# Another order of the seven products, and of their three banks, in the first half of a feed-forward block

## The chip, the cores and the metric

The kernel runs on one core of one Trainium2 chip. A core has five engines with a queue of instructions each: PE (TensorE, matrix products), DVE (VectorE), ACT (ScalarE), POOL (GpSimd) and SP (which here only issues transfers). A product's result goes to PSUM, a small memory of eight banks that PE writes and that ACT and DVE read[...]. The metric is the time of one execution on the device in microseconds (us); lower is better.

## The reference

Thresholded attention (8 sequences, 8 heads, 576 tokens, 64 numbers a head), then a feed-forward block with an ELU between its two products. All data are 32-bit floats.

```python
scores = scale * np.matmul(q, k.transpose(0, 1, 3, 2))
thresh = np.max(scores, axis=-1, keepdims=True) - tau
scores = np.where(scores >= thresh, scores, -1000000000.0)
attn = np.exp(scores - np.max(scores, axis=-1, keepdims=True))
attn = attn / (np.sum(attn, axis=-1, keepdims=True) + 1e-09)
x = (attn @ v)          # then (B,H,S,D) -> (B*S, H*D) = 4608 x 512

h = x @ w_in            # 512 x 2048
g = np.where(h > 0.0, h, alpha * (np.exp(np.minimum(h, 0.0)) - 1.0))
out = g @ w_out         # 2048 x 512
```

## The kernel before, in words

Attention comes in 32 pairs of heads, each in five steps of up to 128 query rows. A step's scores go to PSUM (line 238); DVE takes the row maximum (line 1070); POOL makes the threshold from it (1074); ACT the exponential's bias and the exponential (1078 and 1080); DVE masks and sums (1089) and takes the reciprocal (1095, 1096); POOL normalizes (274). DVE and transfers turn the weights round (348, 361), and PE multiplies them with the values (384, 388).

The feed-forward block is computed in groups of 512 tokens. From the second group on, both its products use a scheme with seven half-size products in place of eight. One group takes eight units of the first product (the function `first_product(g, u)`), with a second round (`second_round`) after each four. A unit multiplies two blocks of 128 hidden columns with 2 x 256 tokens: seven short products, each of two matrix multiplications that appear as four records of 128x256 on PE (line 847). They go to three banks, called place 0, 1 and 2 in the code: `three` takes the next three banks from the list `ends`, and `ends.extend(...)` says in which order the next unit gets them. Until the attention ends there are three such banks for all units (`ends` holds just these); in the tail after it there are six.

In the order before, with k the number of the product (its slot) in the unit:

- k = 0, 1, 2 start places 0, 1 and 2. After each of them ACT copies the bank out (line 861: w, u, s), and POOL adds the copies up (line 866).
- k = 3 adds to place 0, and ACT copies the result out (line 906); k = 4 adds to place 1, and ACT copies it out (line 907). POOL makes t from that copy (line 866, t<-g,u).
- k = 5 adds a21 times x6 to place 0. DVE adds the bank to s and has one quarter of the hidden values (line 869, g<-f,s: the s-add).
- k = 6 adds a12 times x7 to place 2. DVE adds it to t and has the last quarter (line 869, g<-f,t: the t-add).

Adding to a bank doesn't clear it: a place goes on with the sum that it holds, and the copy in between reads what it holds so far. So a product that adds to a place must wait until the copy out of this place is done. The quarters are joined in pairs, halves c = 0 and c = 1. `exp(1)` takes the exponential of half 1 (line 875), and POOL subtracts one (line 889); `exp(0)` takes it of half 0 (line 875), and ACT subtracts one (line 880). Then DVE makes the ELU (line 895) and POOL sums of blocks (line 932), which the second round reads. The t-add completes half 0, the s-add half 1.

What sets the order of all this: the engines' queues are filled in the order in which the program text calls them. An agenda orders it: `on_pe` puts work on PE and advances a clock by a planned cost (0.87 us for a product), and `at(t, f)` puts a follow-up into the agenda at a planned time. The list `after_` holds for each product its follow-ups with their lags behind the product's end. These times only decide the order in each queue; on the chip an instruction starts when its engine is free and what it waits for is done. The attention steps put their work into the same agenda, so a changed lag can move an instruction past the softmax of a step.

In the second round the third product of a part reuses the bank of the first, which ACT copies out before (line 996).

Of the kernel before, what the change touches and what calls it, by code (L numbers as in the profile page):

```python
# [19 lines left out]
def kernel(  # L20
# [436 lines left out]
    def bank():  # L457
        return psum["f"].tile([P, 512], FP32, name="f", tag="f")
# [219 lines left out]
    def blocks_in(u):  # L678
        f0, f1 = (slice(f * P, (f + 1) * P) for f in (u, NU + u))
        return w_in_sb[:, :2, f0], w_in_sb[:, 2:, f0], w_in_sb[:, :2, f1], w_in_sb[:, 2:, f1]  # L680
# [65 lines left out]
    with tc.manual_schedule():  # L746
# [51 lines left out]
        def at(t, f):  # L798
            serial[0] += 1
            heapq.heappush(agenda, (t, serial[0], f))  # L800
# [15 lines left out]
        ends = [bank() for _ in range(3)]  # L816
# [3 lines left out]
        def kept(name):  # L820
            return epool.tile([P, HM], FP32, name=name)
# [4 lines left out]
        def first_product(g, u):  # L826
            r, v = divmod(u, RU)
            (b11, b12), (b21, b22) = ([xts[g][:, k : k + 2, t : t + CT] for t in (0, CT)] for k in (0, 2))
            a11, a12, a21, a22 = blocks_in(u)
            x1, x6, x7 = in_sums["x", g]  # L830
            loc = {}

            def product(k):
                if k == 0:
                    three = [ends.pop(0) for _ in range(3)]
                    ends.extend((three[1], three[0], three[2]))
                    loc["banks"] = [x[:, :CT] for x in three]
                    loc["s"] = in_sums.pop(u)
                    if v == 0:
                        for c in range(2):  # L840
                            gs[g, r, c] = more[r, c] if (r, c) in more else gpool.tile([P, RU, 2, 2, P], FP32, name="g", bufs=2)
                s = loc["s"]
                left, right, place, begins = ((s[:, 1], b22, 0, True), (s[:, 2], b11, 1, True), (s[:, 0], x1, 2, True),
                                              (a11, b12, 0, False), (a22, b21, 1, False), (a21, x6, 0, False),
                                              (a12, x7, 2, False))[k]
                for j in range(2):
                    nc.tensor.matmul(loc["banks"][place], left[:, j], right[:, j], start=(begins and j == 0), stop=(j == 1),  # L847
                                     skip_group_check=True)

            def h(j, c):  # L850
                return gs[g, r, c][:, v, j].rearrange("p i t -> p (i t)")

            def both(c):
                return gs[g, r, c][:, v].rearrange("p j i t -> p (j i t)")

            def place(x):
                return loc["banks"][x]

            def copy(name, x):
                loc[name] = kept(name)  # L860
                nc.scalar.copy(loc[name], place(x))  # L861

            def pool(name, x, other, op):
                if name not in loc:
                    loc[name] = kept(name)
                nc.gpsimd.tensor_tensor(loc[name], x(), loc[other], op)  # L866

            def add(o, x, name):
                nc.vector.tensor_tensor(o, place(x), loc[name], ALU.add)  # L869

            def exp(c):
                while len(late_elus) > 1:
                    late_elus.pop(0)[1]()
                e = loc["e", c] = late["x"].tile([P, 2 * CT], FP32, name="ge", bufs=2)
                nc.scalar.activation(e, both(c), AF.Exp)  # L875
                if c:
                    loc["e1"] = e
                    at(now[0] + 0.75, minus)
                else:
                    nc.scalar.activation(e, e, AF.Copy, bias=-1.0)  # L880
                if attending[0] and (v < RU - 1 or c):
                    late_elus.append((now[0] + 0.7 * c, lambda: elu(c)))
                else:
                    at(now[0] + 1.4, lambda: elu(c))

            def minus():
                e = loc.pop("e1", None)
                if e is not None:
                    nc.gpsimd.tensor_scalar(e, e, 1.0, -1.0, ALU.mult, ALU.add)

            def elu(c):
                if c:
                    minus()

                nc.vector.scalar_tensor_tensor(both(c), loc["e", c], 0.0, both(c), ALU.min, ALU.max)  # L895
                ready.add((g, r, c, v))
                if v % 2:
                    sums(g, r, c, v - 1)

            nm = lambda x: lambda: loc[x]  # L900
            after_ = (
                [(0.1, lambda: copy("w1", 0))],
                [(0.1, lambda: copy("u2", 1)), (0.55, lambda: pool("u2", nm("u2"), "w1", ALU.add))],
                [(0.1, lambda: copy("s1", 2)), (0.6, lambda: pool("s1", nm("s1"), "u2", ALU.subtract)),
                 (0.15, lambda: next_in(g, u))],
                [(0.1, lambda: nc.scalar.copy(h(0, 1), place(0)))],  # L906
                [(0.1, lambda: nc.scalar.copy(h(1, 0), place(1))),
                 (0.55, lambda: pool("t5", lambda: h(1, 0), "u2", ALU.subtract))],
                [(0.1, lambda: add(h(1, 1), 0, "s1")), (1.4 if attending[0] else 0.7, lambda: exp(1))],
                [(0.1, lambda: add(h(0, 0), 2, "t5")), (0.7, lambda: exp(0))],  # L910
            )
            return [(lambda k=k: product(k), after_[k]) for k in range(7)]

        def next_in(g, u):
            x = first_order.index((g, u)) + 2
            if x < len(first_order):
                load_in(first_order[x][1])

        def sums(g, r, c, v):
            def one(k):  # L920
                gt = gs[g, r, c][:, v : v + 2]
                (a11, a21), (a12, a22) = ([gt[:, :, j, i] for i in range(2)] for j in range(2))
                if (r, c, k) in more:
                    cur[g, r, c, k] = more[r, c, k]
                if (g, r, c, k) not in cur:
                    cur[g, r, c, k] = late["x"].tile([P, RU, P], FP32, name=f"s{k}", bufs=1 if k else 2)
                s1, s2, s3, s4 = (cur.get((g, r, c, x)) for x in range(4))
                s1, s2, s3, s4 = (x if x is None else x[:, v : v + 2] for x in (s1, s2, s3, s4))
                o, x, y, op = ((s1, a21, a22, ALU.add), (s2, s1, a11, ALU.subtract),
                               (s3, a11, a21, ALU.subtract), (s4, a12, s2, ALU.subtract))[k]  # L930
                engine = nc.gpsimd if attending[0] or k == 2 else nc.vector
                engine.tensor_tensor(o, x, y, op)  # L932

            for k in range(4):
                job = (0.8, (g, r, c, k), lambda k=k: one(k))

                if c and k and (r, c, k) not in more and (g, r, k) not in ready:
                    waiting.setdefault((g, r, k), []).append(job)
                else:
                    extra.append(job)  # L940
# [108 lines left out]
        def group(g):  # L1049
            for r in range(2):  # L1050
                for u in range(RU * r, RU * r + RU):
                    queue.append((first_product, (g, u)))
                queue.append((second_round, (g, r)))
# [127 lines left out]
        for f in sums_x(B - 1, xs):  # L1181
# [3 lines left out]
        late_sums = sums_x(B, xs)  # L1185
        a, z = B - 1, B
        order = [*((first_product, (a, u)) for u in range(5)), (second_round, (a, 0)),
                 *((first_product, (a, u)) for u in range(5, 8)), (first_product, (z, 0)), (second_round, (a, 1)),
                 *((first_product, (z, u)) for u in range(1, 5)), (second_round, (z, 0)),
                 *((first_product, (z, u)) for u in range(5, 8)), (second_round, (z, 1))]  # L1190
# [42 lines left out]
```

## Time and profile before

| | |
|---|---|
| time, median of 3 runs | 1444.41 us (1440.46 to 1444.94) |
| the profiled execution: time, span | 1436.22 us, 1434.4 us |
| TensorE clock granted in it | 0.995 |
| line 847, waits for ACT's copy 906, PE and its weight loads | 12.3 and 21.9 us, 24 each |
| line 847, waits for ACT's copy w (861), the same | 9.2 and 17.1 us |
| line 847, waits for DVE's adds 869, the same | 6.2 and 15.2 us |

The span is the time from the first to the last instruction of the program in the profiled execution; its time as a run is 1.8 us longer. The profile names an engine, the source line, the operation, and the tiles as result<-inputs with buffer numbers left out. In a timeline a row has its start in us, its length in us, engine, line, operation and tiles, how many instructions were merged into it, and in brackets how long the engine stood idle ahead of it and who released it. PEld is PE's loading of weights, which runs ahead of the product, so one wait appears on both.

### The profile page before, as it was taken

How to read it: one execution, taken by the hardware profiler on the slowest of the kernel's cores; microseconds unless marked ns; L12 is line 12 of the kernel's file. 1: busy time of each engine (PE TensorE's matmuls, PEld its weight loads, DVE VectorE, ACT ScalarE, POOL GpSimd, SP SyncE). 2: the span in 40 equal slices, each digit the busy share in tenths (PEclk: the TensorE clock that was granted, in tenths of full speed). 3: DMA queues.
4: the chain of work that ended last, by engine and by line, in shares of the span. 5: the costliest groups of instructions: out<-in, count | busy, mean ns of one | idle time of the engine just before them, and what ended most of it. 6: DMA issues, size and time to landing. Idle time of an engine off the chain costs nothing.

```text
span 1434.4 us, 21970 instructions
## 1 busy us (share of the span) xinstructions
PE 1350.1 (94%) x6566; PEld 982.9 (69%) x6566; DVE 1062.4 (74%) x2362; ACT 636.8 (44%) x1387; POOL 830.3 (58%) x1331
## 2 busy tenths in 40 slices
PE   6897989998999999999999999999999999999997
PEld 4455646646667677776767676767676777888886
DVE  6778885987778877888788877888778875445433
ACT  5576664235353445445443635363544452323421
POOL 5567774877556564756466647665565646424422
PEclk9999999999999999999999999999999999999999
DMA  5244352798687878788888878787878775421311
GB/s 111 56 104 144 123 131 52 231 262 242 189 243 219 251 205 230 206 249 231 228 223 224 243 217 228 216 252 209 240 219 250 205 230 169 130 67 48 104 56 30
DMA packets 316630, 260.61 MB, mean 182 GB/s; under 512 B 208352, under 2 KB 272352, under 8 KB 316512
## 3 DMA queue, kind: packets, MB, share of 16 engines
q1 hardware_dynamic: 316512, 259.21, 64.2%
q8 instruction: 53, 0.87, 0.3%
q14 instruction: 65, 0.53, 0.1%
HBM read 168.62 MB, written 90.51 MB: 181 GB/s over the span
## 4 chain that ended last, share of the span: by engine, by line
PE 55%; DVE 17%; ACT 8%; issue 6%; POOL 5%; DMA 4%; SPq 3%; DVEq 0%; ACTq 0%; POOLq 0%
PE f L991 21%; PE f L847 12%; PE sc L238 9%; PE pv L388 7%; DVE w L1089 3%; DVE mx L1070 3%; ACT e L1080 2%; DVE x L348 2%; PE pv L384 2%; POOL w L274 2%; PE f L435 2%; DVE w L265 2%; DMA km<-in_k_dram 1%; ACT e L253 1%; SPq L361 1%
## 5 line engine op out<-in xcount | busy, mean ns | idle before, releaser
L274 POOL TENSOR_SCALAR w<-w,rs 128x576 f32<-128x576 f32 x288 | 258.4, 901 | 151.2 <-DVE rs L1096 113.6
L1070 DVE TENSOR_REDUCE mx<-sc 128x1 f32<-128x576 f32 x207 | 148.0, 752 | 82.4 <-PE sc L238 82.4
L238 PE MATMUL sc<-kT,qT 64*128 64x288 f32 x1024 | 181.9, 439 | 23.5 <-DVE w L265 13.0
L348 DVE STREAM_TRANSPOSE x<-w 128x512 f32<-128x512 f32 (+1 forms) x350 | 181.1, 566 | 0.0
L1089 DVE SCALAR_TENSOR_TENSOR w<-sc,th,e 128x576 f32<-128x576 f32 x207 | 162.1, 811 | 18.6 <-POOL th L1074 9.9
L1080 ACT ACTIVATE e<-sc,nb,keep 128x576 f32<-128x576 f32 x207 | 172.0, 831 | 7.0
L238 PEld LDWEIGHTS sc<-kT,qT 64*128 64x128 f32 x1024 | 100.3, 190 | 88.4 <-issue 52.2
L1078 ACT ACTIVATE nb<-mx,nkeep 128x1 f32<-128x1 f32 x207 | 60.8, 293 | 213.9 <-DVE mx L1070 213.9
L847 PE MATMUL f<-xt,w_in_sb 128*128 128x256 f32 x512 | 130.4, 390 | 10.2 <-ACT w L861 9.2
L847 PE MATMUL f<-xt,sw 128*128 128x256 f32 x512 | 126.8, 387 | 2.7 <-DMA sw<-win_sums 2.1
L875 ACT ACTIVATE ge<-g 128x512 f32<-128x512 f32 x112 | 70.4, 630 | 132.2 <-DVE g L869 93.4
L1074 POOL TENSOR_SCALAR th<-mx,ntau 128x1 f32<-128x1 f32 x207 | 54.7, 264 | 115.3 <-DVE mx L1070 113.4
L847 PEld LDWEIGHTS f<-xt,w_in_sb 128*128 128x128 f32 x512 | 92.7, 189 | 41.1 <-ACT w L861 17.1
L847 PE MATMUL f<-x,w_in_sb 128*128 128x256 f32 x448 | 108.3, 385 | 12.3 <-ACT g L906 12.3
L991 PE MATMUL f<-w_out_sb,g 128*128 128x256 f32 x448 | 108.6, 385 | 5.8 <-ACT s L996 5.6
L847 PEld LDWEIGHTS f<-xt,sw 128*128 128x128 f32 x512 | 94.1, 190 | 28.6 <-issue 7.9
L253 ACT ACTIVATE e<-sc,nb,keep 128x576 f32<-128x576 f32 x81 | 65.2, 831 | 105.4 <-POOL nb L249 104.4
L866 POOL TENSOR_TENSOR u<-u,w 128x256 f32<-128x256 f32 x64 | 48.8, 762 | 109.1 <-ACT u L861 105.6
L991 PE MATMUL f<-w_out_sb,s 128*128 128x256 f32 x448 | 109.4, 387 | 0.0
L991 PE MATMUL f<-t,s 128*128 128x256 f32 x448 | 107.0, 381 | 2.3 <-POOL s L932 2.3
L895 DVE SCALAR_TENSOR_TENSOR g<-ge,g 128x512 f32<-128x512 f32 x112 | 89.4, 825 | 22.9 <-ACT ge L880 17.0
L847 PEld LDWEIGHTS f<-x,w_in_sb 128*128 128x128 f32 x448 | 83.1, 190 | 32.2 <-ACT g L906 21.9
(159 smaller groups left out, 2573.1 us busy)
## 6 DMA issues: line engine op xcount, KB each, us to landing
there<-x SPq DMA_DIRECT2D x500, 144.0 KB, 4.0
wTb<-there SPq DMA_DIRECT2D x75, 576.0 KB, 4.7
wTa<-there SPq DMA_DIRECT2D x50, 576.0 KB, 4.2
sw<-win_sums SPq DMA_DIRECT2D x64, 384.0 KB, 4.3
t<-wout_sums SPq DMA_DIRECT2D x45, 512.0 KB, 4.4
qm<-in_q_dram SPq DMA_DIRECT2D x128, 72.0 KB, 2.9
km<-in_k_dram SPq DMA_DIRECT2D x128, 72.0 KB, 4.4
vm<-in_v_dram SPq DMA_DIRECT2D x64, 128.0 KB, 2.5
```

The source lines that it names most:

```text
L238: nc.tensor.matmul(scs[h][:, a, :HALF], qs[r], kT[r, k0 : k0 + HALF], start=True, stop=True)
L253: nc.scalar.activation(e, st[h][:, :, :HALF], AF.Exp, bias=st["nb"][:, h : h + 1], scale=keep)
L274: nc.gpsimd.tensor_scalar(wv, wv, st["rs"][:, h : h + 1], 1.0, ALU.mult, ALU.mult)
L348: nc.vector.transpose(x[:, :, c0 : c0 + nc_], src.rearrange("p (c g n) -> p g c n", c=nc_, n=T))
L388: nc.tensor.matmul(pv[h * D : (h + 1) * D, g0 * T : g1 * T], vm[:, h, c], wT[:, g0:g1, h * (NC + 1) + c], start=False, stop=(c == NC - 1), ...
L847: nc.tensor.matmul(loc["banks"][place], left[:, j], right[:, j], start=(begins and j == 0), stop=(j == 1), skip_group_check=True)
L875: nc.scalar.activation(e, both(c), AF.Exp)
L895: nc.vector.scalar_tensor_tensor(both(c), loc["e", c], 0.0, both(c), ALU.min, ALU.max)
L991: nc.tensor.matmul(place(m), lhs, rhs, start=(begins and v == 0), stop=(v == RU - 1), skip_group_check=True)
L1070: nc.vector.tensor_reduce(st["mx"][:, h : h + 1], st[h][:, :, :HALF], axis=AX.XY, op=ALU.max)
L1080: nc.scalar.activation(e, st[h][:, :, :HALF], AF.Exp, bias=st["nb"][:, h : h + 1], scale=keep)
L1089: nc.vector.scalar_tensor_tensor(wv, sc[:, :, :HALF], st["th"][:, h : h + 1], e, ALU.is_ge, ALU.mult, accum_out=st["sm"][:, h : h + 1])
```

## The change

The last two products of a unit change places: a12 times x7, which adds to place 2, is now k = 5, and a21 times x6, which adds to place 0, is k = 6. Their follow-ups go along with them: the t-add and `exp(0)` now belong to k = 5 with lags of 0.85 and 1.5, the s-add and `exp(1)` to k = 6 with the lags they had. The next unit gets the three banks in another order: first the one of place 1, then that of place 2, then that of place 0. So a unit uses its places in the order 0, 1, 2, 0, 1, 2, 0, and between any two uses of a bank, across units too, two other products stand. Amount and kind of the work stay the same.

```diff
@@ product(k)
                     three = [ends.pop(0) for _ in range(3)]
-                    ends.extend((three[1], three[0], three[2]))
+                    ends.extend((three[1], three[2], three[0]))
...
                 left, right, place, begins = ((s[:, 1], b22, 0, True), (s[:, 2], b11, 1, True), (s[:, 0], x1, 2, True),
-                                              (a11, b12, 0, False), (a22, b21, 1, False), (a21, x6, 0, False),
-                                              (a12, x7, 2, False))[k]
+                                              (a11, b12, 0, False), (a22, b21, 1, False), (a12, x7, 2, False),
+                                              (a21, x6, 0, False))[k]
@@ after_
                  (0.55, lambda: pool("t5", lambda: h(1, 0), "u2", ALU.subtract))],
+                [(0.85, lambda: add(h(0, 0), 2, "t5")), (1.5, lambda: exp(0))],
                 [(0.1, lambda: add(h(1, 1), 0, "s1")), (1.4 if attending[0] else 0.7, lambda: exp(1))],
-                [(0.1, lambda: add(h(0, 0), 2, "t5")), (0.7, lambda: exp(0))],
             )
```

## Prediction

> **What bounds the kernel now.** I read the page first (busy shares, chain), then the groups of line 847, then the timeline of one period.
>
> ```profile
> PE 1350.1 (94%) x6566; PEld 982.9 (69%) x6566; DVE 1062.4 (74%) x2362; ACT 636.8 (44%) x1387; POOL 830.3 (58%) x1331
> PE 55%; DVE 17%; ACT 8%; issue 6%; POOL 5%; DMA 4%; SPq 3%; DVEq 0%; ACTq 0%; POOLq 0%
> L847 PE MATMUL f<-x,w_in_sb 128*128 128x256 f32 x448 | 108.3, 385 | 12.3 <-ACT g L906 12.3
> ```
>
> PE is busy nearly throughout, yet the chain leaves it for 45% of the span: at places the other engines release PE late. The third line is the wait that the change addresses.
>
> From 318 us to 1195 us the work repeats with a period of 76.65 us (slot 0 of a unit at 627.75, 704.41, 781.05): four units, A to D, then one second round, beside ten attention steps. There are 12 such periods. I work in the one from 704.41. All 24 waits of 847 for 906 lie in units B and D (the first period's are a little smaller). End of A, then B:
>
> ```profile
> 712.19 0.42 DVE L869 TENSOR_TENSOR g<-f,t 128x256 f32<-128x256 f32 x1 [1.56 <-POOL t L866]
> 712.71 0.63 ACT L875 ACTIVATE ge<-g 128x512 f32<-128x512 f32 x1 [1.36 <-DVE g L869]
> 713.37 0.63 ACT L880 ACTIVATE ge<-ge 128x512 f32<-128x512 f32 x1
> 713.90 0.35 ACT L861 COPY w<-f 128x256 f32<-128x256 f32 x1
> 714.15 0.29 ACT L1078 ACTIVATE nb<-mx,nkeep 128x1 f32<-128x1 f32 x1
> ...
> 715.21 0.36 ACT L861 COPY u<-f 128x256 f32<-128x256 f32 x1
> ...
> 716.53 0.36 ACT L861 COPY s<-f 128x256 f32<-128x256 f32 x1
> 716.78 0.38 ACT L906 COPY g<-f 128x256 f32<-128x256 f32 x1
> ...
> 717.22 1.99 PE L847 MATMUL f<-x,w_in_sb 128*128 128x256 f32 x8 [0.46 <-ACT g L906]
> ```
>
> Look at ACT: from 712.71 to 717.44 it runs without a gap, so every copy out of a bank here comes as early as ACT allows. B to C:
>
> ```profile
> 719.61 0.63 ACT L875 ACTIVATE ge<-g 128x512 f32<-128x512 f32 x1 [2.17 <-DVE g L869]
> 720.96 0.63 ACT L875 ACTIVATE ge<-g 128x512 f32<-128x512 f32 x1 [0.72 <-DVE g L869]
> 721.62 0.63 ACT L880 ACTIVATE ge<-ge 128x512 f32<-128x512 f32 x1
> 722.15 0.28 ACT L1078 ACTIVATE nb<-mx,nkeep 128x1 f32<-128x1 f32 x1
> 723.20 0.36 ACT L861 COPY w<-f 128x256 f32<-128x256 f32 x1
> 723.61 1.13 PE L847 MATMUL f<-xt,w_in_sb 128*128 128x256 f32 x4 [0.44 <-ACT w L861]
> ```
>
> One exponential (719.61) stands in an idle stretch of ACT; the next (720.96) starts a second burst, whose copy holds PE at C's slot 3. D and the second round behind it:
>
> ```profile
> 738.30 1.99 PE L847 MATMUL f<-x,w_in_sb 128*128 128x256 f32 x8 [0.58 <-ACT g L906]
> 742.17 0.41 DVE L869 TENSOR_TENSOR g<-f,t 128x256 f32<-128x256 f32 x1
> 744.00 0.69 DVE L895 SCALAR_TENSOR_TENSOR g<-ge,g 128x512 f32<-128x512 f32 x1 [1.42 <-ACT ge L880]
> 747.50 0.36 ACT L996 COPY s<-f 128x256 f32<-128x256 f32 x1
> 747.91 1.99 PE L991 MATMUL f<-w_out_sb,g 128*128 128x256 f32 x8 [0.49 <-ACT s L996]
> ```
>
> After D's wait PE soon waits again, for a copy of the second round.
>
> **What the Trainium skill says.** "Perfetto Trace Analysis", section Optimizing Tensor Performance: independent matmul groups should rotate through PSUM banks, so that the evacuation of one overlaps the next one's matmuls. The trace agrees: the one reuse with a single product between waits 0.46 to 0.58 us. "PSUM — Partial Sum Buffer", Summary: guard by bank while another engine reads; here the product starts at 717.22, 0.06 us after copy 906 ended (717.16). "Perfetto Trace Analysis", Sequencer Loop: an instruction waits for its semaphores in its engine's queue; so the place of an exponential in ACT's queue counts, as the unbroken run from 712.71 shows. Section Optimizing Scalar/DVE Operations: GpSimd and VectorE share an SBUF port; in the trace POOL's normalization takes 1.61 us beside VectorE's line 895 at 717.91 and 0.73 otherwise.
>
> **The change part by part.** A product starts 0.86 us after the one before (713.89 to 714.75).
>
> *1. The wait removed.* B's slot 5 should start at 714.75 + 2 x 0.86 = 716.48 and starts at 717.22; D's at 735.83 + 1.73 = 737.56 and starts at 738.30. Each is 0.74 late; gross 24 x 0.74 = 17.8 us. In A and C attention work lies between and there is no such wait.
>
> *2. What is late next in B.* Slot 5 now writes bank 2, whose reader is the copy s (716.53 to 716.89), directly ahead of 906 in ACT's queue. So slot 5 could start at 716.95: 0.27 gained, not 0.74.
>
> *3. The exponentials change places.* Before, exp(1) follows the s-add early (A: 710.72, ACT idle 1.02 before it). After, the built order on ACT is exp(0), line 880, copy w, exp(1), then the softmax: exp(0) still waits for the t-add (712.19, itself waiting for POOL's t), so both exponentials now fall behind it. exp(1) enters ACT's unbroken run in B and pushes the rest by 0.53 (713.37 to 713.90, start to start of such an instruction). Copy u ends at 716.10, slot 4 starts about 0.52 late; copy s ends at 717.42, slot 5 starts at 717.48. B is 0.26 later than before, not earlier. The cover it had, ACT's idle, is gone.
>
> *4. B to C.* The second head's e is 0.53 later, so its mask, the reciprocal and POOL's normalization are (the mask starts 0.10 after e ends today, hence 0.47 counts); POOL's t behind that moves from 719.68 to 720.15 and the t-add from 720.44 to 720.91. exp(0) 721.43, line 880 722.09, exp(1) 722.62, nb 723.15 against 722.15: 1.00 later = 0.47 + 0.53. Queued behind are e and copy w; C's slot 3 starts at 724.61 against 723.61. The s-add, now behind the t-add, delays the row maximum by another 0.34; ACT is later anyway, so that is covered.
>
> *5. C to D.* Value products and scores follow slot 3 on PE, and VectorE waits 0.56 for those scores, so 1.00 passes on. D's slot 1 now needs the t-add (before: slot 2). VectorE's built order there is mask, t-add, mask, s-add: t-add 732.35 to 732.77 on the old clock, slot 1 at 732.83 (+0.48); s-add until 733.81, slot 2 at 733.87 against 733.89. Net nothing.
>
> *6. D.* Slot 5 gains its 0.74: the copies s and 906 are early enough there. But the second round's third product waits for copy 996, whose chain is not PE's: row maximum 744.61, elu 744.00, line 880 743.34, exp(0) 742.68, t-add 742.17, two elus 740.50, s-add 740.18. The s-add now goes behind the t-add, so this starts 0.32 sooner. About 0.3 is kept, 0.4 becomes a longer wait for 996.
>
> *7. A to B.* B's slot 1 (712.92, after scores) now needs the t-add's bank, free at 712.61: 0.25 of slack, cost nothing. If POOL's t slips past that, up to 0.3 a period.
>
> *8. The tail from 1230 us* (16 units, six banks). Units at 1297 and 1395 wait 0.93 for copy w; exp(1) ahead of it adds about 0.5 each. The last second round waits 1.94 at 1406.07 for an elu of half 0, whose exp(0) moves from 1403.46 to about 1402.9 and whose elu escapes the stretched 1.23: about 1.1 sooner. Together nothing.
>
> Per period 1.00 - 0.30 = +0.7; 12 periods +8.4. Against the profiled execution's own time: span 1434.4 to 1442.8, time 1436.2 to 1444.6. The median shown, 1444.4, stands 8.2 above that execution; the same addition gives **1452.8**. SP's queue keeps its order. The trace shows no exp(1) in these places; bounds: at best only C's 0.53 stays, +0.2 a period (+2.4); at worst the 0.3 of D goes and A to B costs 0.3, +1.3 (+15.6).
>
> **Rivals.** (a) *Faster: the waits removed are banked.* Mechanism: PE at slot 5 of B and D, in a stretch where PE is the bound. Price: D 0.74 and B 0.27 = 1.0 a period, 12 us, 1432; with all 0.74 twice, 1427. For it: PE at 94%. Against: ACT's unbroken run in B and the 996 wait behind D. It decides if exp(1) finds gaps in ACT, or if copy w at C comes less than 0.3 later. (b) *No change:* B's delay is taken up in C's slots 0 to 2 (PE waits 0.44 there anyway) and C's slot 3 loses only 0.3 to 0.5, which D returns: 1444 to 1446. (c) *Worse:* t-adds waiting at the head of VectorE hold the s-add, row maximum and softmax in three units of four, and POOL's bound (line 1074), now behind line 889 that waits for exp(1), delays masks too: 1.5 to 2 a period, 1462 to 1468. (d) *The change doesn't do what it says:* two products lie between uses, yet slot 5 of B waits for ACT still; that is inside my forecast.
>
> **How the numbers follow.** Forecast 0.50 (own range 1446.8 to 1460), (a) 0.18, (b) 0.22, (c) 0.10. A change under 0.3% (4.3 us) can't be told from none: faster is below 1440.1, slower above 1448.7. (a) gives faster 0.18; (b) and the forecast's lowest part give same 0.24; the rest, slower 0.58. The range runs from 1438, inside (a), to 1461: outside are most of (a) and of (c), under 0.2 with a share of (a) inside.
>
> **What would show it.** Right: 847's wait for 906 gone; PE waiting in B for copies u and s; C's slot 3 waiting about 1.4 instead of 0.44; the period near 77.35; the wait for 996 near 0.9. Wrong: a period under 76.4, exp(1) in a gap of ACT, or large waits of slot 1 for the t-add.

## The result, and the profile after

The changed kernel takes 1453.75 us (median of 4 runs, 1452.9 to 1456.14); the kernel before took 1443.05 in the runs beside it (4 runs, 1440.46 to 1444.94). The ratio is 1.0078, 95% interval 1.0056 to 1.010: slower by 10.7 us.

The profiled execution of the changed kernel has a span of 1451.2 us, 16.8 above that of the kernel before. I cut both at the first short product of unit 0 and of unit 48, where the tail begins. All times in the table come from the starts of line 847 on PE; a period alternates between a longer and a shorter kind.

| stretch, us | before | after | difference |
|---|---|---|---|
| up to the first short product | 318.15 | 325.49 | +7.3 |
| the twelve periods | 912.36 | 917.75 | +5.4 |
| one period, longer and shorter kind | 76.67 / 75.97 | 77.24 / 76.56 | +0.57 / +0.59 |
| the tail | 203.85 | 208.01 | +4.1 |

The first row isn't the change: up to there both kernels hold the same program. The table by stretch of the two profiles (time, busy us of each engine with its instructions, PEclk, DMA share, GB/s) shows another clock in the stretch ahead of that product. Before:

```profile
200.00:318.10 118.10, 110.44 (x482) 65.22 (x482) 90.48 (x189) 40.56 (x76) 77.12 (x117) 1.00 0.57 166
```

After:

```profile
200.00:325.40 125.40, 116.46 (x489) 67.33 (x487) 92.98 (x193) 43.44 (x81) 79.76 (x121) 0.96 0.56 160
```

From 200 us to the first short product PE's clock was 0.96 instead of 1.00, and the stretch took 125.4 us instead of 118.1. This belongs to the one execution: in the twelve other traces of this document the same instructions up to there take 318.9 to 325.5 us. The change itself is +5.4 and +4.1, together +9.5, near the 10.7 of the medians.

The page of the changed kernel, its chain of waits and two groups of line 847:

```profile
PE 45%; DVE 20%; ACT 11%; POOL 9%; issue 8%; DMA 4%; SPq 3%; DVEq 0%; ACTq 0%; POOLq 0%
L847 PE MATMUL f<-xt,w_in_sb 128*128 128x256 f32 x512 | 132.2, 390 | 26.1 <-ACT w L861 21.1
L847 PE MATMUL f<-x,w_in_sb 128*128 128x256 f32 x448 | 107.1, 382 | 2.1 <-ACT s L861 2.1
```

The wait for the copy 906, 12.3 us before, is gone: the group that had it waits 2.1 us, for copy s. But the wait for copy w went from 9.2 to 21.1 us, and PE's share of the chain from 55% to 45%: more of the path now leads through the other engines. The timeline of the period from 713.35 us (704.41 before; so 8.94 lies between the two clocks), units B, C and D:

```profile
722.29 0.63 ACT L880 ACTIVATE ge<-ge 128x512 f32<-128x512 f32 x1
722.83 0.35 ACT L861 COPY w<-f 128x256 f32<-128x256 f32 x1
723.08 0.63 ACT L875 ACTIVATE ge<-g 128x512 f32<-128x512 f32 x1
723.61 0.28 ACT L1078 ACTIVATE nb<-mx,nkeep 128x1 f32<-128x1 f32 x1
...
725.07 1.13 PE L847 MATMUL f<-xt,w_in_sb 128*128 128x256 f32 x4 [0.36 <-ACT u L861]
...
726.39 1.99 PE L847 MATMUL f<-x,w_in_sb 128*128 128x256 f32 x8 [0.19 <-ACT s L861]
...
731.60 0.61 ACT L875 ACTIVATE ge<-g 128x512 f32<-128x512 f32 x1
732.12 0.28 ACT L1078 ACTIVATE nb<-mx,nkeep 128x1 f32<-128x1 f32 x1
...
733.58 1.13 PE L847 MATMUL f<-xt,w_in_sb 128*128 128x256 f32 x4 [1.22 <-ACT w L861]
...
750.41 1.36 DVE L895 SCALAR_TENSOR_TENSOR g<-ge,g 128x512 f32<-128x512 f32 x2
751.69 0.41 DVE L869 TENSOR_TENSOR g<-f,t 128x256 f32<-128x256 f32 x1
...
757.02 0.36 ACT L996 COPY s<-f 128x256 f32<-128x256 f32 x1
757.43 1.99 PE L991 MATMUL f<-w_out_sb,g 128*128 128x256 f32 x8 [0.63 <-ACT s L996]
```

In B the second exponential stands between copy w and the softmax's bias (723.08), so PE waits for u at slot 4 and for s at slot 5. In C it stands ahead of nb (731.60), and slot 3 waits 1.22 for w instead of 0.44. In D no product waits for ACT; the second round's wait for copy 996 is 0.63 instead of 0.49.

### The profile page after: what moved, and what is told of

The parts are those of the page before. It is cut to its first block, busy times and chain, and to the rows that moved or that the text cites. A ratio compares the mean times of both kernels' runs of the same rounds, so it can differ in the third digit from the quotient of the medians.

```text
span 1451.2 us, 21921 instructions
## 1 busy us (share of the span) xinstructions
PE 1359.4 (94%) x6566; PEld 984.4 (68%) x6566; DVE 1066.0 (73%) x2362; ACT 630.2 (43%) x1387; POOL 842.8 (58%) x1331
## 4 chain that ended last, share of the span: by engine, by line
PE 45%; DVE 20%; ACT 11%; POOL 9%; issue 8%; DMA 4%; SPq 3%; DVEq 0%; ACTq 0%; POOLq 0%
PE f L991 20%; PE sc L238 7%; PE pv L388 6%; PE f L847 6%; DVE w L1089 3%; POOL w L274 3%; ACT ge L875 3%; ACT e L1080 3%; DVE mx L1070 2%; DVE x L348 2%; DMA km<-in_k_dram 2%; PE f L435 2%; PE pv L384 2%; DVE w L265 2%; DVE g L869 1%
## 5 line engine op out<-in xcount | busy, mean ns | idle before, releaser
L274 POOL TENSOR_SCALAR w<-w,rs 128x576 f32<-128x576 f32 x288 | 268.4, 935 | 157.4 <-DVE rs L1096 118.4
L1070 DVE TENSOR_REDUCE mx<-sc 128x1 f32<-128x576 f32 x207 | 148.0, 752 | 76.8 <-PE sc L238 75.9
L847 PE MATMUL f<-xt,w_in_sb 128*128 128x256 f32 x512 | 132.2, 390 | 26.1 <-ACT w L861 21.1
L847 PE MATMUL f<-xt,sw 128*128 128x256 f32 x512 | 130.4, 390 | 8.8 <-DVE g L869 7.3
L847 PEld LDWEIGHTS f<-xt,sw 128*128 128x128 f32 x512 | 92.2, 189 | 40.2 <-DVE g L869 16.8
L991 PEld LDWEIGHTS f<-w_out_sb,g 128*128 128x128 f32 x448 | 82.8, 190 | 28.2 <-ACT s L996 11.8
L889 POOL TENSOR_SCALAR ge<-ge 128x512 f32<-128x512 f32 x64 | 39.5, 618 | 105.3 <-ACT ge L875 105.3
```

Of the source, the lines that this page charges most:

```text
L274: nc.gpsimd.tensor_scalar(wv, wv, st["rs"][:, h : h + 1], 1.0, ALU.mult, ALU.mult)
L991: nc.tensor.matmul(place(m), lhs, rhs, start=(begins and v == 0), stop=(v == RU - 1), skip_group_check=True)
L1070: nc.vector.tensor_reduce(st["mx"][:, h : h + 1], st[h][:, :, :HALF], axis=AX.XY, op=ALU.max)
```

## The experiments

"New follow-ups" means the order in which the changed kernel queues them: t-add and exp(0) ahead of s-add and exp(1). "Old follow-ups" means that of the kernel before. Each kernel's runs are set against runs of the kernel before on the same chip; its median there was 1441.8 to 1443.5. Positions in a period are counted from slot 0 of its unit A in the period of unit 20, a shorter one: 75.97 us before, 76.55 after.

| kernel | ratio, 95% interval | period, longer / shorter | tail |
|---|---|---|---|
| before | | 76.67 / 75.97 | 203.9 |
| the change | 1.0078, 1.0056 to 1.010 | 77.24 / 76.56 | 208.0 |
| E1 new products, old follow-ups | 1.0068, 1.0046 to 1.009 | 76.93 / 76.22 | 211.7 |
| E2 old products, new follow-ups | 1.0127, 1.0099 to 1.0155 | 77.25 / 76.55 | 216.5 |
| E6 new products, new follow-ups in D | 0.9992, 0.998 to 1.0005 | 76.35 / 75.65 | 208.4 |
| E7 old products, new follow-ups in D | 0.9954, 0.9943 to 0.9966 | 75.96 / 75.25 | 206.2 |
| E8 as E7, tail as before | 0.994, 0.9923 to 0.9957 | 75.98 / 75.28 | 205.4 |
| E10 the change, tail as before | 1.0042, 1.0028 to 1.0056 | 77.27 / 76.59 | 205.4 |
| E9 the change, exp(1) of A to C later, tail as before | 0.9887, 0.9872 to 0.9901 | 75.17 / 74.46 | 203.7 |
| E11 as E9, old products in D | 0.9925, 0.9912 to 0.9938 | 75.67 / 74.97 | 203.7 |
| E12 as E9, old products and rotation | 0.9996, 0.9982 to 1.0011 | 76.50 / 75.80 | 205.4 |
| E13 as E12, new rotation | 0.9908, 0.9886 to 0.9931 | 75.65 / 74.96 | 203.7 |

E3 and E4 were run once each, so they have no ratio: 1460.05 and 1442.22 us.

### The two halves of the change apart: E1 and E2

E1 is the changed kernel with the follow-ups back in the old order.

```diff
-                [(0.1, lambda: add(h(1, 1), 0, "s1")), (1.4 if attending[0] else 0.7, lambda: exp(1))],
+                [(-0.03, lambda: add(h(1, 1), 0, "s1")), (0.53 if attending[0] else -0.02, lambda: exp(1))],
```

> The changed kernel, but the lags of the s-add and exp(1) are set so that VectorE does the s-add ahead of the t-add and ACT exp(1) ahead of exp(0), as before the change; products and banks stay as changed. Theory A (the loss lies in the order of the follow-ups, and the waits removed are worth little): as before, 0 to +0.2 us a period of 76.67, ratio to before 1.000 to 1.003, the wait for copy 996 rising by about 0.7 a period. Theory B (the waits removed are banked by PE, only the follow-ups spoil it): 12 us faster, ratio 0.992. Theory C (the banks and products themselves cost, for the t-add's bank is wanted one product sooner): as slow as the changed kernel, 1.007.

The period is 0.26 longer than before. B's slot 5 starts at 12.55 instead of 12.81 and waits only 0.19, for copy s; but C's slot 3 starts at 19.22 (19.20 before), where it now waits 0.70 for w instead of 0.44. D's slot 1 waits 0.90 for the t-add, which the s-add precedes, and slot 2 starts 0.5 late; slot 6 is 0.44 early, and the second round's third product waits 0.74 for 996. So of the waits removed nothing arrives. (On VectorE the old order isn't restored everywhere: in D, for instance, the two adds of C stand between the two masks, where before the s-add stood ahead of both and the t-add behind them. On ACT and POOL the order is the old one throughout.) In the tail most units take 6.47 us or more instead of 6.04: there the s-add, now of slot 6, comes one slot later, and copy w stands on ACT behind the exponentials that follow it. So the period came near theory A, but the ratio, 1.0068, is beyond its 1.003, because the tail is 7.8 us longer.

E2 is the kernel before with the new follow-ups and the new rotation of banks, so on ACT, DVE and POOL the order is that of the changed kernel.

```diff
-                    ends.extend((three[1], three[0], three[2]))
+                    ends.extend((three[1], three[2], three[0]))
...
-                [(0.1, lambda: add(h(1, 1), 0, "s1")), (1.4 if attending[0] else 0.7, lambda: exp(1))],
-                [(0.1, lambda: add(h(0, 0), 2, "t5")), (0.7, lambda: exp(0))],
+                [(0.97, lambda: add(h(1, 1), 0, "s1")), (2.27 if attending[0] else 1.57, lambda: exp(1))],
+                [(-0.02, lambda: add(h(0, 0), 2, "t5")), (0.63, lambda: exp(0))],
```

> The kernel before in its products (a21 x6 in slot 5, so the wait for copy 906 is back), but with the changed kernel's order of follow-ups (t-add ahead of s-add, exp(0) ahead of exp(1)) and its order of banks for the next unit. Theory A: within 2 us of the changed kernel, ratio to before 1.006 to 1.009; D waits 0.74 for copy 906 again and the wait for 996 shrinks by as much. Theory B: the waits come on top, 9 to 12 us slower than the changed kernel, 1.014 to 1.016. Theory C: as before, 1.000.

Its periods are those of the changed kernel to 0.01 us, although both waits for 906 are back:

```profile
726.67 1.99 PE L847 MATMUL f<-x,w_in_sb 128*128 128x256 f32 x8 [0.46 <-ACT g L906]
...
733.58 1.13 PE L847 MATMUL f<-xt,w_in_sb 128*128 128x256 f32 x4 [0.96 <-ACT w L861]
...
748.53 1.99 PE L847 MATMUL f<-x,w_in_sb 128*128 128x256 f32 x8 [0.58 <-ACT g L906]
```

C's slot 3 (the second row) starts 20.23 us into the period in both kernels, and in E2 the wait for 996 isn't there at all. So beside the new follow-ups the order of the products is worth nothing in the periods: the two removed waits are paid back at C's slot 3 and in the second round. The +0.58 of a period comes with the follow-ups and the new rotation, which E2 has both; these follow-ups with the old products and the old rotation were not run.

As a whole E2 missed theory A: the ratio is 1.0127 instead of 1.006 to 1.009. The tail makes the difference. It is 8.5 us longer than in the changed kernel, with the same order on ACT, DVE and POOL: there most units take 6.47 us or more instead of 6.04, since both adds now wait for slot 6. (2.4 of the 8.5 lie behind the start of the last unit, where PEclk was 0.94 instead of 0.99.) So in the tail, beside these follow-ups, the new order of the products does help.

### The follow-ups unit by unit: E6, E7 and E8

E6 is the changed kernel with old follow-ups in A to C (v is the unit within its four, RU - 1 the last, D). E7 is the kernel before with new follow-ups in D.

```diff
@@ E7
-                [(0.1, lambda: add(h(1, 1), 0, "s1")), (1.4 if attending[0] else 0.7, lambda: exp(1))],
-                [(0.1, lambda: add(h(0, 0), 2, "t5")), (0.7, lambda: exp(0))],
+                [(0.97 if v == RU - 1 else 0.1, lambda: add(h(1, 1), 0, "s1")), ((2.27 if attending[0] else 1.57) if v == RU - 1 else (1.4 if attending[0] else 0.7), lambda: exp(1))],
+                [(-0.02 if v == RU - 1 else 0.1, lambda: add(h(0, 0), 2, "t5")), (0.63 if v == RU - 1 else 0.7, lambda: exp(0))],
```

> As e1, but the last unit ahead of each second round (D) keeps the changed kernel's follow-ups: t-add, then s-add, exp(0) ahead of exp(1). Theory A: the second round's copy 996 comes 0.3 to 0.7 us sooner a period, and PE, no longer waiting at D's slot 5, can use it: -0.2 to -0.6 a period, and about -1 at the end of the tail: ratio 0.994 to 0.997. Theory C: no better than the changed kernel, 1.007.

> The kernel before, with only the follow-ups of D in the changed order; products and banks as before, so every wait for copy 906 stays. Theory A (what D saved in the changed kernel comes from the order on VectorE and ACT, not from the wait removed): -0.4 to -0.7 a period and -1 in the tail, ratio 0.993 to 0.996. Theory B (it comes from the wait removed): as before, 0.999 to 1.000.

In D the new follow-ups gain: 0.71 a period with the old products (E7 against before), 0.57 with the new ones (E6 against E1). In A to C they lose 0.89 (the change against E6). E7 keeps both waits for 906 and is still shorter than before, since the wait for 996 is gone. E6 missed its ratio, 0.994 to 0.997: its tail is 4.6 us longer than before, where about 1 us less was expected. E7's tail is 2.3 us longer, which E8 takes up: the same only while attention work is queued. The first of its two lines:

```diff
@@ E8, against E7
-                [(0.97 if v == RU - 1 else 0.1, lambda: add(h(1, 1), 0, "s1")), ((2.27 if attending[0] else 1.57) if v == RU - 1 else (1.4 if attending[0] else 0.7), lambda: exp(1))],
+                [(0.97 if attending[0] and v == RU - 1 else 0.1, lambda: add(h(1, 1), 0, "s1")), ((2.27 if v == RU - 1 else 1.4) if attending[0] else 0.7, lambda: exp(1))],
...
```

> The kernel before, with the follow-ups of unit D alone put into the new order, and only in the units in which attention work is still queued; the last 16 units (the tail) keep the old order. Theory A (the gain of e7_old_products_new_queues_in_d lies in unit D of the periods, and its loss of 2.3 us in the tail comes from the same follow-ups where no attention work stands between them): the periods are 0.7 us shorter each as there, about 906.8 us for twelve, and the tail is back at 203.9 us, so the ratio is 0.994 to 0.9955, a little below that of e7. Theory B (the tail of e7 is chance of one execution): the same ratio as e7, 0.9954, and a tail of about 206.

The ratio is as expected and the tail shorter than in E7, but in this execution still 1.6 above before. All of it lies behind the start of the last unit, where ACT, DVE and POOL have the order of the kernel before, and there PEclk was 0.94 instead of 0.98. E10 and E12 show the same 1.7 at the end; E9, E11 and E13, with the same tail, don't.

### The tail: E10

The change in the periods, the kernel before in the last 16 units: `new` is set when a unit's work is queued and true while attention work is left.

```diff
@@ E10, against before
-            loc = {}
+            loc, new = {}, attending[0]
...
-                    ends.extend((three[1], three[0], three[2]))
+                    ends.extend((three[1], three[2], three[0]) if attending[0] else (three[1], three[0], three[2]))
...
```

> The changed kernel while attention work is queued, the kernel before in the last 16 units. Theory A (the 4.1 us that the tail got longer come from the change's follow-ups there: both elus and their sums ahead of the t-add): periods as in the changed kernel, 917.75 us, tail as in the kernel before, 203.9 us, so the time is about 4 us under that of the changed kernel and the ratio to the kernel before 1.004 to 1.005. Theory B (the tail's difference is that of two executions): ratio 1.0078 as the changed kernel.

1.0042 instead of 1.0078: the tail's loss is the change's own. (The two intervals just touch, but in E10's trace each unit of the tail takes what it took before, to 0.15 us, up to the last one.) Where it lies, the two timelines show. Before:

```profile
1390.69 0.69 DVE L895 SCALAR_TENSOR_TENSOR wTa<-ge,wTa 128x512 f32<-128x512 f32 x1 [0.60 <-POOL ge L889]
...
1395.54 0.84 DVE L932 TENSOR_TENSOR e<-wTb,km 128x256 f32<-128x256 f32 x1
...
1399.12 1.13 PE L847 MATMUL f<-xt,w_in_sb 128*128 128x256 f32 x4 [0.93 <-ACT w L861]
```

After:

```profile
1407.76 0.69 DVE L895 SCALAR_TENSOR_TENSOR wTb<-ge,wTb 128x512 f32<-128x512 f32 x1 [0.89 <-ACT ge L880]
1408.98 1.20 DVE L895 SCALAR_TENSOR_TENSOR wTa<-ge,wTa 128x512 f32<-128x512 f32 x1 [0.53 <-POOL ge L889]
1410.11 0.94 DVE L932 TENSOR_TENSOR qm<-wTb 128x256 f32<-128x256 f32 x1
...
1414.14 0.42 DVE L932 TENSOR_TENSOR w<-wTa,vm 128x256 f32<-128x256 f32 x1
1414.49 0.42 DVE L869 TENSOR_TENSOR wTb<-f,t 128x256 f32<-128x256 f32 x1
...
1416.71 0.35 ACT L861 COPY w<-f 128x256 f32<-128x256 f32 x1
...
1417.12 1.13 PE L847 MATMUL f<-xt,w_in_sb 128*128 128x256 f32 x4 [2.08 <-ACT w L861]
```

Behind every second unit VectorE makes two elus and sums of blocks (line 932) ahead of the next unit's adds. In the kernel before, half 1's elu came first (1390.69) and its three sums followed at once, then elu and sums of half 0: the last ended at 1396.38, 0.94 us after slot 0 of the last unit (1395.44). Now the exponential of half 1 comes second and waits longer, both elus stand ahead of all six sums, and VectorE is idle for 0.89 and 0.53 on the way. The last sum ends at 1414.56, 2.28 after that slot 0 (1412.28), and behind it come t-add, the exponentials and copy w. PE waits 2.08 us at this slot 3 (0.93 before), and 0.65 in two units that didn't wait before. This is read from the timelines; no run takes the row of sums apart from the rest of the change.

### Where the exponential of half 1 may stand: E3, E4

E3 moves the s-add ahead of the t-add and leaves ACT as in the changed kernel; E4 leaves VectorE's adds and queues exp(1) later.

```diff
@@ E3
-                [(0.1, lambda: add(h(1, 1), 0, "s1")), (1.4 if attending[0] else 0.7, lambda: exp(1))],
+                [(-0.03 if attending[0] else 0.1, lambda: add(h(1, 1), 0, "s1")), (1.4 if attending[0] else 0.7, lambda: exp(1))],
@@ E4
-                [(0.1, lambda: add(h(1, 1), 0, "s1")), (1.4 if attending[0] else 0.7, lambda: exp(1))],
+                [(0.1, lambda: add(h(1, 1), 0, "s1")), (5.6 if attending[0] else 0.7, lambda: exp(1))],
```

> The changed kernel with the s-add back ahead of the t-add in the units with attention; the order on the ScalarE is untouched, so the exponential of the second half still stands directly behind that of the first, within the unbroken run of unit B. Theory A (what costs is the exponential's place in the ScalarE's run): unit B's slot 4 still starts 11.7 us after the period's start, unit C's slot 3 still at about 20.2, and the period is 77.2 us or more on one side of the alternation, up to 77.5, as what unit D saved by its s-add order is lost in part. Theory B (what costs is the s-add's place on the VectorE): the period falls to about 76.7.

> The changed kernel with the exponential of the second half queued later while attention is queued: on the ScalarE it stands behind the copies of s and of the first half's hidden product instead of ahead of them. Theory A (what costs is the exponential's place in the ScalarE's run): unit B's slot 4 is back at 11.2 us after the period's start, slot 5 at about 12.5, unit C's slot 3 at about 19.2, and the period falls to 76.2 to 76.5 us (0.25 more between units C and D, 0.7 less in D than the kernel before). Theory B (the loss is elsewhere): the period stays at 77.2.

E3: B's slot 4 at 11.73, C's slot 3 at 20.23, as in the changed kernel, and the period 77.70, 0.2 beyond what I had allowed. The s-add's place isn't the cost in B and C; in D it is worth 0.46, of which 0.34 comes behind slot 6.

E4: C's slot 3 falls to 18.98, sooner than in the kernel before (19.20), so the exponential's place is the cost in B and C (with its elu on VectorE, which moves along with it, see E9). But slot 4 of B starts at 11.50, not 11.2, since exp(0) there starts at 8.58 and not at 8.28; and the period is 76.62, above the 76.2 to 76.5 expected: D's exponential now stands behind copy 996, its elu comes late, and PE waits 1.39 for it in the second round.

### Both together: E9 and E11

So exp(1) should stand behind the copies in A to C and early in D. E9 is the changed kernel with just that, and the tail as before:

```diff
@@ E9, against E10
-                    ends.extend((three[1], three[2], three[0]) if attending[0] else (three[1], three[0], three[2]))
+                    ends.extend((three[1], three[2], three[0]) if new else (three[1], three[0], three[2]))
...
-                *([[(0.85, lambda: add(h(0, 0), 2, "t5")), (1.5, lambda: exp(0))], [(0.1, lambda: add(h(1, 1), 0, "s1")), (1.4, lambda: exp(1))]] if new else
+                *([[(0.85, lambda: add(h(0, 0), 2, "t5")), (1.5, lambda: exp(0))], [(0.1, lambda: add(h(1, 1), 0, "s1")), (1.4 if v == RU - 1 else 5.6, lambda: exp(1))]] if new else
```

> The changed kernel's products, banks and follow-ups while attention is queued, but in units A to C the exponential of the second half is queued behind the copies of s and of the first half's hidden product, and in unit D it stays where the changed kernel has it; the last 16 units are as in the kernel before. Theory A (the parts of e4_exp_behind_copies add up: up to D's slot 6 its 70.70 us of a 76.62 us period instead of 71.93 of the changed kernel's 77.24 on the same count, and behind D the changed kernel's second round): the period is 76.0 and 75.3 us in turn, 0.65 under the kernel before, the ratio 0.993 to 0.9955. Theory B (with units A to C sooner, the second round is released by the attention work or by the elu of the first half at the same time as in e4): the period stays at 76.6 and 76.0, the ratio at 0.998 to 1.001.

1427.07 us, ratio 0.9887: the shortest of all, and 0.8 us a period better than I had added up. Its timeline, from 706.42 us:

```profile
715.92 0.35 ACT L861 COPY w<-f 128x256 f32<-128x256 f32 x1
716.17 0.29 ACT L1078 ACTIVATE nb<-mx,nkeep 128x1 f32<-128x1 f32 x1
...
719.07 0.65 ACT L875 ACTIVATE ge<-g 128x512 f32<-128x512 f32 x1
...
719.94 0.67 DVE L895 SCALAR_TENSOR_TENSOR g<-ge,g 128x512 f32<-128x512 f32 x1
720.13 1.09 POOL L274 TENSOR_SCALAR w<-w,rs 128x576 f32<-128x576 f32 x1 [0.33 <-DVE rs L1096]
...
741.87 0.76 DVE L895 SCALAR_TENSOR_TENSOR g<-ge,g 128x512 f32<-128x512 f32 x1
742.55 0.41 DVE L869 TENSOR_TENSOR g<-f,t 128x256 f32<-128x256 f32 x1
```

The first two rows: the softmax's bias follows copy w directly. The exponential comes after the copies (719.07), and its elu therefore later too. That has a second effect, which I hadn't counted: where two elus stood beside POOL's normalization in B (line 895 for 1.27 us, line 274 for 1.61, at 717.91 and 718.10 before), one stands there now, and the normalization takes 1.09. POOL's t, the t-add, exp(0) and copy w follow it, and C's slot 3 starts at 18.70, 0.50 sooner than before. In D one elu instead of two stands ahead of the t-add (0.76 us instead of 1.36), and the wait for copy 996 falls to 0.07.

E11 gives unit D the old products and rotation again, with its follow-ups as in E8:

```diff
@@ E11, against E9
-            loc, new = {}, attending[0]
+            loc, new, last = {}, attending[0] and v < RU - 1, attending[0] and v == RU - 1
...
```

> As e9_change_with_exp_behind_copies, but unit D has the old products and the old rotation of banks behind it, with its follow-ups in the new order, as in e8_new_queues_in_d_attending_only. Theory A (D with old products and new follow-ups takes 48.89 us from its slot 0 to the period's end, as in e7, against 49.13 with the new products; units A to C take 26.85 as in e4): the period is 75.74 and 75.05 us in turn, the ratio 0.991 to 0.9935, the shortest of all. Theory B (unit A of the next period, which now gets a bank that D used last, or one of D's waits takes the gain): 76.0 us or more, the ratio at or above 0.994.

The period and the ratio are those of theory A, but it isn't the shortest of all: it is 0.50 a period longer than E9. D's slot 5 waits 0.58 for copy 906 again (33.64 instead of 32.90), and here this wait has to be paid.

### What the products are worth then: E12 and E13

E12 has the queues of ACT, DVE and POOL of E9 and the old products and rotation on PE; E13 the old products alone.

```diff
@@ E12, against before
-            loc = {}
+            loc, new = {}, attending[0]
...
-                [(0.1, lambda: add(h(1, 1), 0, "s1")), (1.4 if attending[0] else 0.7, lambda: exp(1))],
-                [(0.1, lambda: add(h(0, 0), 2, "t5")), (0.7, lambda: exp(0))],
+                [(0.97 if new else 0.1, lambda: add(h(1, 1), 0, "s1")), ((2.27 if v == RU - 1 else 6.47) if new else 0.7, lambda: exp(1))],
+                [(-0.02 if new else 0.1, lambda: add(h(0, 0), 2, "t5")), (0.63 if new else 0.7, lambda: exp(0))],
@@ E13, against E12
-                    ends.extend((three[1], three[0], three[2]))
+                    ends.extend((three[1], three[2], three[0]) if new else (three[1], three[0], three[2]))
```

> The queues of ScalarE, VectorE and GpSimd exactly as in e9_change_with_exp_behind_copies, with the old order of products and the old rotation of banks on PE; so it differs from e9 by what the change does to PE alone. Theory A (once no exponential stands ahead of a copy that PE waits for, the removed waits are worth time: 0.27 in unit B, where slot 5 waited for the copy 906 behind the copy s, and 0.50 in unit D, as between e11_old_products_in_d and e9): both waits for 906 are there, the period is 75.9 and 75.2 us in turn, the ratio 0.994 to 0.9965. Theory B (PE's order is worth nothing, as between the changed kernel and e2_old_products_new_queues; the whole gain of e9 is the exponentials' place): the period is 75.2 and 74.5, the ratio 0.9875 to 0.990.

> As e12_old_products_exp_behind_copies, but the next unit gets the banks in the changed kernel's order (places 1, 2, 0); so it differs from e9_change_with_exp_behind_copies only in which of the last two products comes first. Theory A (of the 1.33 us a period that e12 lies above e9, the wait of unit D's slot 1 for the s-add, 1.63 instead of 0.57, is the old rotation's, and the rest is what the two waits for the copy 906 cost): D's slot 1 waits 0.57 again, both waits for 906 stay (0.46 and 0.58), the period is 75.9 and 75.2 us, the ratio 0.994 to 0.9965. Theory B (the wait of slot 1 only stands where another would, and the whole 1.33 is the products' order): 76.5 and 75.8, the ratio 0.998 to 1.001. Theory C (the products' order is worth nothing and all of it was the rotation): 75.2 and 74.5, the ratio 0.9875 to 0.990.

E12's period is 76.50, which neither theory gave. The rows of its unit D:

```profile
737.57 0.42 DVE L869 TENSOR_TENSOR g<-f,t 128x256 f32<-128x256 f32 x1
737.90 0.81 DVE L1089 SCALAR_TENSOR_TENSOR w<-sc,th,e 128x576 f32<-128x576 f32 x1
...
738.64 0.42 DVE L869 TENSOR_TENSOR g<-f,s 128x256 f32<-128x256 f32 x1
...
739.11 0.70 PE L847 MATMUL f<-xt,sw 128*128 128x256 f32 x2 [1.63 <-DVE g L869]
```

With the old rotation D's slot 1 takes the bank that C's s-add reads, and the s-add now stands behind the t-add and a mask. With the new rotation (E13) slot 1 takes the t-add's bank and waits 0.56. E13 comes to 75.65, between what the expectation called A (75.9) and C (75.2): the rotation is 0.85 of the 1.33, the products' order 0.48. B's share of that is nothing (slot 5 starts at 12.82 against E9's 12.54, but C's slot 3 at 18.69 against 18.70); all 0.48 is D's. There the chain to copy 996 has become PE's: the row maximum waits for the scores, and starts 12.57 us after D's slot 0 in E13, 11.99 in E9; the copy starts at 15.47 and at 15.00. So with the queues of E9 the part of the change that lies on PE, products and rotation together, is worth 1.33 us a period.

## Why the prediction was right, and where its terms were off

The time was 1453.75 against 1452.8, and slower as forecast. Some of that nearness is luck: the forecast stood on 1444.4 for the kernel before, which took 1443.05 in the runs beside the change; the loss is 10.7, forecast were 8.4. By the steps:

- **1, wait removed:** it is. Gross 17.8 us, net nothing in the periods (E2).
- **2, copy s is late next in B:** slot 5 waits 0.19 for s. E1, without the exponential in the way, gains the 0.26, and C takes it back.
- **3, exp(1) enters ACT's run:** on the old clock slot 4 starts at 716.13 and slot 5 at 717.45; predicted were 0.52 late, so 716.15, and 717.48. The Trainium skill, "ScalarE: Activation LUTs", section What ACT_TABLE_LOAD costs, gives an ACTIVATE without pointer operands 186 ns and 0.833 ns an element, and 93 ns of overlap back to back: an estimate of 612 and 519 ns for 512 elements. The trace has 0.63 and 0.53.
- **4, B to C:** on the same clock t starts at 720.19 (predicted 720.15), the t-add at 720.95 (720.91) and C's slot 3 at 724.64 (724.61). E3 and E4 show the exponential's place as its cause, not the s-add's. The Trainium skill, "PSUM — Partial Sum Buffer", section Engine vs sequencer instructions, calls the queues of ScalarE, VectorE and GpSimd strict FIFO, first in, first out; these runs agree: in B the bias nb starts at 723.61, behind the exponential of 723.08, though the row maximum that it reads, the first of two, had ended by 722.71.
- **5, C to D, net nothing: off.** Slot 1 starts at 734.10 (predicted 732.83 + 1.00 = 733.83) and slot 2 at 735.17 (734.87). This hand-over costs 0.25. The prediction moved VectorE's mask up to where the s-add had begun (731.64; with C's delay of 1.04, 732.68), but it starts at 732.89, after 0.14 us in which VectorE stands idle.
- **6, D keeps 0.3: off.** From D's slot 2 on 0.71 is kept. 0.32 is the s-add's, as said; E3, with the s-add first again, loses 0.34 behind D's slot 6. The other 0.39 wasn't foreseen: the two elus ahead of the t-add take 1.36 us instead of 1.75. Before, the s-add stood ahead of them, and POOL's normalization began first; now the elus begin first, and it is the normalization that gets longer (rows below). The misses of steps 5 and 6 partly cancel: 1.04 + 0.25 - 0.71 = 0.58 a period, predicted 0.70. The twelve together make 5.4, not 8.4, as each is smaller and the first period became 0.74 shorter. (The first period is 80.2 to 84.4 us in the traces of this document, so that part may be chance.) The prediction also read the period as 76.65; that is the longer of two kinds, and the next slot 0 is at 780.39, not 781.05.
- **7, A to B:** no wait there, as said.
- **8, the tail, together nothing: wrong.** The two gains and losses named are there: the waits for w grew by 1.15 each instead of 0.5, and the last second round waits 0.81 instead of 1.94. The prediction counted the exponential ahead of copy w, 0.5, and not the row of sums on VectorE, which now begins behind both elus and holds the t-add. New waits for w in two more units (0.65 and 0.64) and one for copy 996 that grew by 1.17 weren't foreseen either. The tail costs 4.1 in the profile; E10's ratio is 0.0036 lower, some 5 us.

The rows of step 6, the first two of the kernel before, the others of the changed one:

```profile
740.36 0.75 POOL L274 TENSOR_SCALAR w<-w,rs 128x576 f32<-128x576 f32 x1
740.50 1.75 DVE L895 SCALAR_TENSOR_TENSOR g<-ge,g 128x512 f32<-128x512 f32 x2
...
750.41 1.36 DVE L895 SCALAR_TENSOR_TENSOR g<-ge,g 128x512 f32<-128x512 f32 x2
750.59 1.71 POOL L274 TENSOR_SCALAR w<-w,rs 128x576 f32<-128x576 f32 x1
```

So the total is right in part by luck: the periods cost 3 us less and the tail 4 more than predicted. The mechanism of B and C came out to 0.05 us; D's and the tail's sizes did not.

Rival (a), waits banked, was rejected for the change as it is, and E2 shows that this was right for the periods. What decides it was named too, "if exp(1) finds gaps in ACT": it is nearly that. E9 puts exp(1) behind the copies that PE waits for, and there the products' order is worth 0.48 a period (E9 against E13). 1427 is also what the rival gave for all waits gained, but E9 gets there largely by another route, the places of exp(1) and of the elus together with the new rotation: E13 has most of the gain with both waits for 906 in place.

Left open: why exp(0) of A starts 0.28 later in E4 than in E9, 0.04 after the s-add's end instead of 0.09 after the t-add's; how much of the profiled executions' difference at their ends is the clock's alone; and what the new rotation costs or gains by itself beside the changed kernel's follow-ups.

## What to carry to other kernels

A reordering on one engine also reorders the queues of those that serve it; price the follow-ups' new places, one engine at a time, before the wait that is to go. Undo each half alone, as here: in the periods the order of the products, which was meant to help, was worth nothing beside the follow-ups that came along with it. With one lag changed the order was worth 0.48 us a period, and with the rotation 1.33. And look behind a wait before counting it: here 0.74 us of waiting was worth nothing where a later product of the same stretch waited for the same chain.

## What was not expected of the hardware

A VectorE elu (128x512) and a GpSimd normalization (128x576) that overlap don't share the delay: which of them gets longer went with which had started first. Where the elu started 0.19 us ahead, it took its usual 0.67 to 0.69, and the normalization took 1.09 beside this one elu, or 1.61 when a second elu followed, instead of 0.73. Where the normalization started 0.14 ahead (740.36), it took 0.75, and the first of the two elus 1.15 instead of 0.69.

So E9, where one of two elus in B stands 7 us later on VectorE, makes an instruction on another engine 0.5 us shorter and PE's next waiting product 0.5 us sooner; and in D the same normalization cost PE's chain 0.39 us more or less, by which of the two engines began first.
